# Three more groups of products on zeros, and another written-out order, in a fused state-space and SiLU kernel

## The chip, the cores and the metric

The kernel runs on one core of one Trainium2 chip. The metric is the device time of one execution in microseconds (us), the median of a few runs. A profile of one further execution gives the traces that are read below; its times are counted from the start of its own span.

## The reference

Two blocks follow each other. The first is a chunked state-space scan over 4 batches, 8 heads, 768 steps, 32 values per head and a state of 16; the second is a two-layer network on the 3072 resulting rows of 256 values.

```python
for c in range(nc):                      # chunks of 32 steps
    cum = np.cumsum(log_a[chunk])
    L  = np.exp(cum[i] - cum[j]) * causal
    y  = (C @ B.T * L) @ x + (C @ state) * np.exp(cum)
    state = decay_full * state + sum_j(B_j x_j * decay_from_j)
x = y.transpose(0, 2, 1, 3).reshape(3072, 256)
h = x @ w_in                             # 256 -> 2048
out = (h * sigmoid(h)) @ w_out           # 2048 -> 256
```

All inputs and the output are float32.

## The kernel before

The 3072 rows are cut into 12 units of 256 rows (three per batch, `UT = 256`), and two units make a pair of 512 rows for the network. The kernel has no loop over them. One string, `SCHEDULE`, holds some 1400 tokens; each token calls one small function, which records a few instructions for one engine. The string is the order of the program: every engine gets its instructions in the order in which the tokens stand, and waits at each for the data that it needs. A second table, `SLOTS`, says which of the numbered buffers each new tile gets (49 small ones `s2k`, 12 large ones `r4k`, 7 `raw` for weights as loaded, 3 accumulators `hp`). Nothing else decides order or place.

The scan of one unit u, with the lines of the profile:

- Loads: `Ln` (L244, B and C by rows), `Lt` (L252, four pieces per tensor in the other layout), `Lx` (L259, x), `La` and `Lp` (L219 and L227, decay factors from a scratch tensor in DRAM). The last number of a token is the queue that issues it: 0 is SP's, 1 is ACT's, 2 is POOL's. A DMA waits until the DMA that used its semaphore last has landed; there are eight such semaphores in rotation, so it waits for the one eight places before it.
- Decay: for units 0 and 1, `ab` (L477) spreads the factors by products on TensorE and `E` (L486) scans them on VectorE (DVE); `E,0,0,1`, `E,0,0,0` and `E,0,1` are unit 0, `E,1,1` and `E,1,0` unit 1. `pb` (L451) and `P01` (L456) do the same for another layout; later units use `P` (L463).
- Operands: `B` (L494, POOL), `T` (L499, a transpose on DVE; `T,0,1` makes C of unit 0 from its four `Lt` pieces), `tp` and `tq` (L505 on TensorE and L514 on ScalarE (ACT), a transpose of B), `ce` (L520, ACT), `C` (L525, mostly POOL).
- Products: `D` or `gd` (L547, B times x), `g0` (L561, C times B), then `M` (L576, DVE, times the decay), `b` and `S` (L570 on ACT and L591 on DVE, the state), `SM` (L599, ACT), and `Y` (L612, then L621, the unit's result), which is copied out by `X0` (L651, units 0 and 1) or `y` (L657).

The network: weights come with `lw` (L278) and are cut into a high and a low part over several steps: `u`, `v`, `H` and `Wd` on ACT (L284, L287, L315, L326), `w` and `Wl` on DVE (L293, L297, L300, L321), `W` and `We` on POOL (L311, L330). The first pair of units uses plain float32 products, `s` and `n` (L681 and L749), with `si` (L687) between; the other five pairs use three products of parts, `a` and `d` (L790) and `f` (L771, each `f,1` is one product of 512 columns), with `ax`, `dg`, `h` on ACT (L801, L811, L817) and `l`, `e` on DVE (L638, L641). Rows leave with `o` (L699) and `O` (L703).

The token that the change adds is `z`: `z,1` is one bfloat16 product of a tile of zeros with itself, 128x512, into the bank `o_ps` (L421), and `z,0,6` is six small ones of 64x64 (L423). Their result is read by nobody; the bank is overwritten by the next `tp`.

```python
def busy(n, little=0):
    t = bank("z")
    for i in range(n):
        nc.tensor.matmul(out=t, lhsT=idle[:, 0:128], rhs=idle, start=True, stop=True)
```

Of the kernel before, what the change touches and what calls it, by code (L numbers as in the profile page):

```python
# [30 lines left out]
n,1 W,10,1,0 lw,12 W,5,1,0 M,2,0 Ln,3,0,0,0 w,11,1 P,2 T,3,1 La,3,0,0 C,2 n,1 b,2,0 W,11,1,0 u,6 La,3,1,0 n,1 S,2,0
w,6,0 s,0,5 w,7,2 Wd,0 b,2,1 Lx,3,1,0 S,2,1 Lt,4,1,0,0 v,6 n,1 Ln,3,0,1,0 u,7 w,7,0 Lt,3,0,1,0 S,2,2 AD,1 ce,3,1 w,7,1
SM,2,0 w,6,1 n,1 H,5 SM,2,1 Lt,3,0,0,0 Lt,3,0,2,0 Lt,3,0,3,0 n,1 Y,2 Lx,3,0,0 si,0,5 w,6,2 E,3,0 E,3,1 y,2,0 W,7,1,0
B,3 u,12 T,3,0 Lp,3,0 n,1 w,12,0 n,1 ce,3,0 H,11 y,2,1 lw,13 La,4,0,0 Lt,4,0,2,0 W,6,1,0 Lt,4,1,2,0 w,12,1 s,0,7 g0,3
gd,3 si,0,7 H,3 s,0,6 b,3,0 P,3 Wl,0 H,7 n,1 M,3,1 Lt,4,1,3,0 Wl,2 S,3,0 La,4,1,0 b,3,1 n,1 S,3,1 v,12 xh,2 si,0,6
S,3,2 Lt,4,0,1,0 Wd,4 Lt,4,0,0,0 x,2,1 M,3,0 s,1,6 Lt,4,1,1,0 SM,3,1 S,3,3 SM,3,0 Lx,4,1,0 C,3 x,2,0 H,6 si,1,6 lw,15
lw,14 Ln,4,0,1,0 w,12,2 W,12,1,0 T,4,1 H,9 Y,3 Ln,4,0,0,0 s,1,5 E,4,1 n,1 u,13 y,3,1 y,3,0 H,8 v,13 xh,3 Lt,4,0,3,0
n,1 Lx,4,0,0 u,15 w,13,0 x,3,0 si,1,5 We,0 a,1,0 AD,2 Lp,4,0 s,1,7 x,3,1 ce,4,0 v,14 ax,1,0 w,13,2 w,13,1 d,1,0 u,14
H,10 n,1 La,5,1,0 w,14,2 W,13,1,0 ce,4,1 n,1 E,4,0 B,4 T,4,0 dg,1,0 Wd,2 Wd,5 g0,4 Lt,5,1,2,0 La,5,0,0 w,14,0 w,14,1
gd,4 b,4,0 b,4,1 Wl,9 P,4 Wd,3 C,4 S,4,0 M,4,0 Wd,10 Lx,5,0,0 S,4,1 w,15,0 M,4,1 Lp,5,0 Lt,5,1,1,0 S,4,2 n,1 W,14,1,0  # L40
v,15 H,14 Lt,5,1,3,0 SM,4,0 n,1 Wl,10 SM,4,1 H,13 Wd,9 n,1 si,1,7 Wl,3 n,1 w,15,2 Wd,1 w,15,1 Y,4 n,2 y,4,0 a,1,2 Wl,1
Ln,5,0,0,0 We,2 h,1,0 n,1 Lt,5,1,0,0 n,1 ax,1,2 y,4,1 e,1,0 W,15,1,0 Wd,8 a,1,1 We,1 La,6,0,0 n,2 Wl,8 We,9 xh,4 n,1
l,1,0 ax,1,1 T,5,1 H,12 f,2 d,1,2 Lt,5,0,1,0 dg,1,2 We,8 d,1,1 dg,1,1 Vn,0 n,1 a,1,4 a,1,3 Lt,5,0,2,0 f,1 Vn,1 S,4,3
f,4 P,5 h,1,1 Wl,5 f,1 Wl,14 We,4 x,4,0 We,10 Ln,5,0,1,0 La,6,1,0 ce,5,0 E,6,0 Lt,5,0,0,0 ax,1,4 ax,1,3 Lx,5,1,0
Lt,6,1,0,0 Wl,12 d,1,4 We,3 Wl,11 Lt,5,0,3,0 x,4,1 d,1,3 T,5,0 f,1 h,1,2 ce,5,1 E,5,0 E,5,1 C,5 Lt,6,1,1,0 f,1 dg,1,4
Lt,6,0,2,0 Lt,6,1,2,0 f,1 e,1,1 f,1 Lt,6,0,3,0 f,1 Lt,6,1,3,0 Lt,6,0,0,0 Lt,6,0,1,0 l,1,1 f,1 B,5 dg,1,3 H,15 g0,5
T,6,1 gd,5 M,5,1 AD,3 Wd,7 We,5 f,1 ce,6,0 b,5,0 f,1 h,1,3 Ln,6,0,1,0 f,1 S,5,0 b,5,1 Ln,6,0,0,0 e,1,2 S,5,1 S,5,2 f,1
Wl,7 a,1,5 M,5,0 l,1,2 f,1 Lp,6,0 h,1,4 f,2 Lt,7,1,2,0 ax,1,5 f,2 Wd,6 f,1 Wd,11 l,1,3 d,1,5 f,1 SM,5,1 f,1 dg,1,5
o,0,0,2 P,6 Wl,6 We,7 f,1 Wd,12 e,1,3 ce,6,1 f,2 l,1,4 f,3 We,11 f,1 We,12 SM,5,0 Y,5 f,1 Lx,6,1,0 T,6,0 Lt,7,1,1,0
f,1 ct y,5,1 E,6,1 Lx,6,0,0 f,1 a,1,7 Lx,7,0,0 e,1,4 f,2 B,6 f,2 y,5,0 Ln,7,0,1,0 ax,1,7 f,1 C,6 f,1 h,1,5 We,6 xh,5  # L50
d,1,7 f,1 Wl,15 f,1 dg,1,7 o,0,1,2 f,1 Lt,7,0,2,0 Wd,15 f,1 Lx,7,1,0 gd,6 Lt,7,1,3,0 g0,6 f,2 M,6,1 x,5,0 Wd,14 Wl,13
f,1 x,5,1 f,1 O,0,0,2,0,0 f,2 b,6,0 b,6,1 M,6,0 f,1 h,1,7 a,2,1 l,1,5 ax,2,1 a,1,6 Wd,13 Lp,7,0 S,6,0 Lt,7,0,0,0 d,2,1
Lt,7,1,0,0 f,1 e,1,5 Lt,7,0,1,0 We,13 f,1 S,6,1 ax,1,6 dg,2,1 l,1,7 La,7,1,0 T,7,1 d,1,6 dg,1,6 ce,7,0 f,1 S,6,2
SM,6,0 f,2 SM,6,1 f,2 h,1,6 f,1 Y,6 l,1,6 S,6,3 f,3 y,6,0 f,1 e,1,6 Lt,8,1,0,0 ce,7,1 P,7 f,3 y,6,1 We,15 La,7,0,0 f,1
# [836 lines left out]
```

## Time and profile before

| what | us |
|---|---|
| median of three runs | 329.32 |
| the three runs | 331.9, 329.31, 329.32 |
| the profiled execution | 327.4 |
| its span in the trace | 325.7 |
| TensorE (PE) busy in the span | 319.0 |
| VectorE (DVE) busy | 235.2 |
| ScalarE (ACT) busy | 207.4 |
| GpSimd (POOL) busy | 69.3 |

The profiled execution lasted 1.7 us longer than its span, which begins with the first instruction and ends with the last. "PEld" is TensorE's loading of stationary operands, which runs beside its products. A product with float32 operands leaves two records, one with bfloat16 or with split parts one. The order of instructions comes from the tokens, so a row of the trace can be matched with its token by line and position.

### The profile page before, as it was taken

What the parts mean: (1) busy time and instruction counts of PE and PEld (TensorE: products, weight loads), DVE (VectorE), ACT (ScalarE), POOL (GpSimd) and SP (SyncE); (2) the same over time, 40 slices, a digit from 0 to 9 for tenths busy, and PEclk for the clock granted to TensorE, in tenths of its full rate; (3) what the DMA queues carried; (4) which work ended last, traced back from release to release, by engine and by line L of the source; (5) the groups of instructions that cost most, each with busy time, mean ns of one, the idle gap of its engine ahead of it and who ended that gap; (6) DMA issues with size and microseconds to landing.
All of it is one profiled execution on the core that took longest, in us unless ns stands there. A gap on an engine that the chain in (4) does not pass through costs nothing.

```text
span 325.7 us, 7539 instructions
## 1 busy us (share of the span) xinstructions
PE 319.0 (98%) x3065; PEld 243.7 (75%) x3065; DVE 235.2 (72%) x330; ACT 207.4 (64%) x321; POOL 69.3 (21%) x88
## 2 busy tenths in 40 slices
PE   8899999999999999999999999999999999999995
PEld 4578656665677777877777878778887888888883
DVE  7968989798987986769386768886567563366373
ACT  2869665877499678655567667645856464864441
POOL 6447375335741422100000101010010000000000
PEclk9999999999999999999999999999999999999999
DMA  7899986945947669340604153143001100003002
GB/s 149 192 318 216 232 184 180 213 122 115 206 82 117 107 136 180 72 70 4 133 16 78 51 112 64 38 82 74 2 0 27 33 0 0 2 13 60 17 1 64
DMA packets 95762, 30.64 MB, mean 94 GB/s; under 512 B 80280, under 2 KB 86936, under 8 KB 95728
## 3 DMA queue, kind: packets, MB, share of 16 engines
q1 hardware_dynamic: 90576, 25.38, 35.7%
q0 software_dynamic: 2480, 4.39, 7.6%
q10 hardware_dynamic: 2672, 0.39, 0.7%
q8 instruction: 24, 0.39, 0.5%
q14 instruction: 10, 0.08, 0.1%
HBM read 22.61 MB, written 3.34 MB: 80 GB/s over the span
## 4 chain that ended last, share of the span: by engine, by line
PE 90%; DVE 3%; DMA 2%; ACT 2%; POOL 1%; issue 1%; POOLq 0%; DVEq 0%
PE hp L771 29%; PE gb L790 17%; PE ga L790 16%; PE hp L681 7%; PE hp L749 7%; PE o_ps L771 6%; DMA s2k<-in_B_dram 2%; PE ga L621 2%; PE ga L561 2%; PE ga L612 2%; PE gb L612 1%; PE ga L547 1%; DVE ab L486 1%; DVE ab L576 0%; DVE s2k L300 0%
## 5 line engine op out<-in xcount | busy, mean ns | idle before, releaser
L771 PE MATMUL hp<-r4k,s2k 128*128 128x512 f32 x400 | 112.9, 394 | 0.0
L771 PEld LDWEIGHTS hp<-r4k,s2k 128*128 128x128 f32 x400 | 74.3, 188 | 16.3 <-issue 0.8
L638 DVE SCALAR_TENSOR_TENSOR r4k<-r4k,r4k 128x1024 fp32r<-128x1024 f32 x40 | 48.7, 1221 | 31.4 <-ACT r4k L817 23.7
L790 PE MATMUL ga<-raw,s2k 128*128 128x512 f32 x240 | 62.7, 396 | 0.0
L641 DVE SCALAR_TENSOR_TENSOR r4k<-r4k,r4k 128x1024 fp32r<-128x1024 f32 x40 | 48.6, 1219 | 19.2 <-ACT r4k L817 13.3
L790 PE MATMUL gb<-raw,s2k 128*128 128x512 f32 x240 | 61.4, 391 | 0.0
L790 PEld LDWEIGHTS ga<-raw,s2k 128*128 128x128 f32 x240 | 44.5, 188 | 11.6 <-issue 0.7
L790 PEld LDWEIGHTS gb<-raw,s2k 128*128 128x128 f32 x240 | 44.7, 188 | 10.6 <-ACT ys L657 0.6
L817 ACT ACTIVATE r4k<-r4k 128x1024 fp32r<-128x1024 f32 x40 | 41.8, 1056 | 2.0 <-DVE r4k L641 1.0
L494 POOL TENSOR_TENSOR BT<-bn,ab 128x256 f32<-128x256 f32 x10 | 10.4, 1042 | 104.4 <-DVE ab L486 83.9
L811 ACT ACTIVATE r4k<-ga 128x1024 f32<-128x1024 f32 x20 | 20.5, 1026 | 18.2 <-PE ga L790 17.5
L801 ACT ACTIVATE ga<-ga 128x1024 f32<-128x1024 f32 x20 | 20.2, 1009 | 18.4 <-PE ga L790 18.4
L801 ACT ACTIVATE gb<-gb 128x1024 f32<-128x1024 f32 x20 | 20.2, 1009 | 18.3 <-PE gb L790 18.3
L771 PE MATMUL o_ps<-r4k,s2k 128*128 128x512 f32 x80 | 31.0, 394 | 0.0
L681 PE MATMUL hp<-r4k,s2k 128*128 128x256 f32 x128 | 29.6, 383 | 0.6 <-ACT r4k L651 0.6
L311 POOL TENSOR_TENSOR s2k<-s2k,s2k 128x512 uint32<-128x512 uint32 (+1 forms) x19 | 24.6, 1300 | 25.3 <-DVE s2k L300 13.8
L749 PE MATMUL hp<-r4k,s2k 128*128 128x512 f32 x64 | 29.8, 598 | 0.0
L486 DVE TENSOR_TENSOR_SCAN ab<-ab,diag 128x512 f32<-128x512 f32 x20 | 27.1, 1372 | 2.9 <-DMA ab<-az 2.9
L681 PEld LDWEIGHTS hp<-r4k,s2k 128*128 128x128 f32 x128 | 23.9, 190 | 5.4 <-issue 1.4
L811 ACT ACTIVATE r4k<-gb 128x1024 f32<-128x1024 f32 x20 | 20.5, 1024 | 6.3 <-PE gb L790 4.5
L749 PEld LDWEIGHTS hp<-r4k,s2k 128*128 128x128 f32 x64 | 11.7, 189 | 10.4 <-issue 9.6
L330 POOL DMA_DIRECT2D s2k<-s2k x16 | 14.2, 1090 | 15.9 <-ACT s2k L326 7.0
(120 smaller groups left out, 382.2 us busy)
## 6 DMA issues: line engine op xcount, KB each, us to landing
ab<-az SPq DMA_DIRECT2D x20, 256.0 KB, 5.5
raw<-in_moe_w_in_dram SPq DMA_DIRECT2D x8, 512.0 KB, 5.1
raw<-in_moe_w_out_dram SPq DMA_DIRECT2D x8, 512.0 KB, 5.9
s2k<-s2k POOLq DMA_DIRECT2D x16, 256.0 KB, 4.7
out_dram<-r4k SPq DMA_DIRECT2D x44, 64.0 KB, 1.8
xt<-in_x_dram SPq DMA_DIRECT2D x20, 128.0 KB, 4.8
pz<-ac SPq DMA_DIRECT2D x10, 130.0 KB
bn<-in_B_dram SPq DMA_DIRECT2D x20, 64.0 KB, 2.5
```

The source lines that it names most:

```text
L311: nc.gpsimd.tensor_tensor(out=dst[:, :, fs].bitcast(U32), in0=u[:, :, fs], in1=v[:, :, fs], op=ALU.add)
L330: nc.gpsimd.dma_start(out=f32(WK[n, p]).rearrange("p k f -> p (k f)"), in_=other.rearrange("p k f -> p (k f)"), accum_op=ALU.add)
L486: nc.vector.tensor_tensor_scan(out=o, data0=src, data1=heads(diag, half).rearrange("p h t -> p (h t)"), initial=0.0, op0=ALU.mult, op1=ALU ...
L638: nc.vector.scalar_tensor_tensor(out=l, in0=f32(h), scalar=BACK, in1=y, op0=ALU.mult, op1=ALU.add)
L641: nc.vector.scalar_tensor_tensor(out=d, in0=f32(h), scalar=-(BACK + 1.0), in1=y, op0=ALU.mult, op1=ALU.subtract)
L681: nc.tensor.matmul(out=hp[:, i], lhsT=WT[j][:, kc, 128 * i:128 * i + 128], rhs=XM[:, 2 * kc:2 * kc + 2, u], start=(kc == 0), stop=(kc == K ...
L749: nc.tensor.matmul(out=NP["o"][m], lhsT=WT[8 + f // 2][:, f % 2, 128 * m:128 * m + 128], rhs=GT[0, f // 2][:, f % 2], start=(f == 0), stop ...
L771: nc.tensor.matmul(out=ACC[P, 2 * (p == "d") + m], lhsT=WK[8 + f // 2, p][:, f % 2, 128 * m:128 * m + 128], rhs=rhs, start=(f == 0 and p ! ...
L790: nc.tensor.matmul(out=o, lhsT=WK[j, q][:, kc, 128 * i:128 * i + 128], rhs=xs[:, 2 * kc:2 * kc + 2], start=(start and q == "h" and kc == 0 ...
L801: nc.scalar.activation(t, t, AF.Copy, scale=1.0 + Z)
L811: nc.scalar.activation(g, t, AF.Silu, scale=BACK)
L817: nc.scalar.activation(t, GT[G, i], AF.Copy, scale=-LESS * Z)
```

## The change

The tokens stand in another order, and three `z,1` are added; every other token is there as often as before (the `f` and `n` groups are cut differently, with the same sums, 480 and 32 products). `SLOTS` gives the tiles other buffers accordingly. The last 485 tokens, from `h,3,1` on, are the same in both.

The beginning before and after, and the two places of `Wl,4`:

```diff
-ch ci cs zr Ln,0,0,0,1 cP cI z,1 z,1 z,1 ia ip,0 z,0,6 Lt,0,1,0,1 c1 cp z,0,6 z,1 A,1 c2 A,0 Lt,0,1,3,1 Lt,0,1,2,1
-PA,0 Lt,0,1,1,1 ab,0,0,1 ab,0,0,0 ab,0,1 Lx,0,1,0 cd Ln,0,0,1,1 PA,1 E,0,0,1 lw,2 u,2 co E,0,0,0 E,0,1 pb,0 T,0,1
-ce,0,0 P01,0 Lx,0,0,0 ce,0,1 B,0,0 B,0,1 z,1 lw,1 ab,1,1 E,1,1 tp,0 tq,0 D,0 g0,0 S,0,0 lw,0 w,2,0 S,0,1 Ln,1,0,0,0
-v,2 M,0,1 u,1 M,0,0 z,0,6 C,0 Ln,1,1,0,0 z,0,6 Ln,1,1,1,0 Ln,1,0,1,0 S,0,2 v,1 w,2,1 SM,0,0 Lx,1,0,0 SM,0,1 ab,1,0
-Lx,1,1,0 w,2,2 lw,3 W,2,2,0 Y,0 u,0 ir,3 W,2,2,1 ir,1 X0,0,0 X0,0,1 lw,4 v,0 ir,0 s,0,2 E,1,0 S,0,3 si,0,2 tp,1 ce,1,0
...
-w,9,0 Ln,2,0,1,0 W,3,1,0 AA,1 s,0,3 La,2,1,0 s,1,3 H,2 La,2,0,0 W,8,1,0 v,10 Wl,4 w,5,0 u,11 Lx,2,1,0 v,9 w,5,1 si,0,3
...
-gd,4 b,4,0 b,4,1 Wl,9 P,4 Wd,3 C,4 S,4,0 M,4,0 Wd,10 Lx,5,0,0 S,4,1 w,15,0 M,4,1 Lp,5,0 Lt,5,1,1,0 S,4,2 n,1 W,14,1,0
+ci cs ia ch ip,0 c1 Ln,0,0,0,1 z,1 cp z,1 zr c2 Lt,0,1,1,1 A,1 z,1 Lt,0,1,2,1 cI Lt,0,1,3,1 z,0,6 z,0,6 Lt,0,1,0,1 z,1
+PA,0 A,0 cP cd ab,0,0,1 ab,0,0,0 E,0,0,1 E,0,0,0 Lx,0,1,0 ab,0,1 Ln,0,0,1,1 T,0,1 E,0,1 pb,0 ab,1,1 PA,1 B,0,0 B,0,1
+P01,0 ce,0,1 ce,0,0 lw,2 E,1,1 z,1 Lx,0,0,0 lw,1 z,1 tp,0 u,2 tq,0 v,2 C,0 D,0 lw,0 S,0,0 g0,0 z,0,6 z,0,6 w,2,0 S,0,1
+Ln,1,1,0,0 M,0,1 M,0,0 Ln,1,0,0,0 Ln,1,0,1,0 S,0,2 Ln,1,1,1,0 u,1 w,2,2 v,1 SM,0,0 w,2,1 SM,0,1 u,0 Lx,1,0,0 Lx,1,1,0
+lw,3 ab,1,0 Y,0 ir,2 W,2,2,0 lw,4 W,2,2,1 E,1,0 ir,1 B,1,0 ir,3 X0,0,0 z,1 z,1 w,0,0 X0,0,1 v,0 w,1,0 B,1,1 s,0,2 ir,0
...
+La,5,0,0 gd,4 w,14,0 w,14,1 Wd,3 b,4,0 Wl,4 b,4,1 Wl,9 P,4 C,4 n,1 W,14,1,0 M,4,1 S,4,0 M,4,0 Lx,5,0,0 S,4,1 Lp,5,0
```

Read engine by engine, the beginning is this. TensorE before: three `z,1`, two `z,0,6`, `z,1`, `ab,0,0,1`, `ab,0,0,0`, `ab,0,1`, `pb,0`, `z,1`, `ab,1,1`, `tp,0`, `D,0`, `g0,0`, two `z,0,6`, `ab,1,0`, `Y,0`, `s,0,2`. After: the same, but `ab,1,1` stands right behind `pb,0`, two `z,1` stand between it and `tp,0`, and two more stand between `Y,0` and `s,0,2`. On DVE the order before is `E,0,0,1 E,0,0,0 E,0,1 T,0,1 P01,0 E,1,1 S,0,0 w,2,0 S,0,1 M,0,1 M,0,0`; after, `T,0,1` stands ahead of `E,0,1`. On ACT the two `ce` of unit 0 come ahead of `u,2`, and the four `Lt` pieces of unit 0 are issued in another order, in the same four places of the queue. The first seven DMAs of SP's queue are the same. Between there and the common tail, some 60 tokens on DVE, 70 on ACT, 15 on TensorE, 10 on POOL and 60 on SP's queue stand a few places earlier or later; `Wl,4` moves from the weights of the first pair to just ahead of `Wl,9` and `P,4`, and `M,4,1` moves ahead of `S,4,0`.

## The prediction

> **What bounds the kernel now.** I read the busy shares first, then the chain that ended last, then TensorE by stages.
>
> ```profile
> PE 319.0 (98%) x3065; PEld 243.7 (75%) x3065; DVE 235.2 (72%) x330; ACT 207.4 (64%) x321; POOL 69.3 (21%) x88
> ...
> PE 90%; DVE 3%; DMA 2%; ACT 2%; POOL 1%; issue 1%; POOLq 0%; DVEq 0%
> ```
>
> ```profile
> 9.20:14.00 4.80, 4.15 (x167) 2.81 (x167) 4.60 (x11) 3.97 (x10) 1.71 (x4) 1.00 0.91 179
> 14.00:60.00 46.00, 45.92 (x527) 32.45 (x528) 40.15 (x71) 33.49 (x70) 25.06 (x26) 1.00 0.89 219
> 60.00:80.00 20.00, 19.86 (x301) 12.60 (x300) 17.00 (x26) 16.27 (x33) 8.91 (x9) 1.00 0.66 150
> 80.00:165.00 85.00, 84.98 (x790) 65.67 (x788) 65.58 (x84) 58.21 (x88) 22.82 (x24) 1.00 0.58 109
> ```
>
> The first number pair of the windows is the stretch, then TensorE's busy time. From 14 us on TensorE idles 0.08 us up to 60, 0.14 up to 80, 0.02 up to 165, and nothing shows until 316: it is the bound, and the amount of its work there is not changed (480 and 480 products of parts, 64 and 32 plain ones). An order of the other engines can lose time there, but gain hardly any. What can be gained lies before 14 us, and that stage is a chain of latencies:
>
> ```profile
> 0.82 2.62 DMA s2k<-in_B_dram
> 3.44 0.02 issue
> 3.46 5.26 DMA s2k<-in_B_dram
> 8.72 0.04 issue
> 8.77 0.33 PE o_ps L505
> ```
>
> The second half of B lands at 8.72 us; TensorE's `tp,0` waits for it, then `D,0` (9.18), `g0,0` (9.64), DVE's `M` (10.51), `Y,0` (11.85), ACT's `X0` (13.40) and `s,0,2` (13.93) follow. From `s,0,2` on TensorE is dense, so a shift of that instruction shifts the end by as much. Both transfers of B keep their places in ACT's queue, so 8.72 stands.
>
> **The change part by part.**
>
> *The zeros cost nothing.* One `z,1` at full speed takes TensorE 0.22 us (6.73 to 6.95 in the rows below).
>
> ```profile
> 6.73 0.39 PE L421 MATMUL o_ps<-s2k 128*128 128x512 bf16 x1
> 6.95 1.02 PE L477 MATMUL hp<-s2k,s2k 128*128 128x512 f32 x2
> 7.81 0.27 PE L505 MATMUL o_ps<-ident,s2k 128*128 128x128 f32 x1
> 8.77 0.33 PE L505 MATMUL o_ps<-ident,s2k 128*128 128x128 f32 x1 [0.68 <-DMA s2k<-in_B_dram]
> ```
>
> After the change `ab,1,1` starts at 6.73 instead of 6.95, ends its turn at 7.59, two zeros take it to 8.04, and the first transpose moves from 7.81 to 8.04. The second still waits for 8.72: 0.68 us of idle time covers the 0.23. If B landed at 7.8 the cost would be 0.23. The other two stand behind `Y,0`, whose last product is issued at 13.16; they take the engine to about 13.65, inside the 0.55 us in which `s,0,2` waits for `X0` (13.38 to 13.93). Cover gone, they would cost 0.45; at half speed (three zeros from 1.27 to 2.66 are 0.46 each) they would take 0.9 and cost about 0.4. I take 0 for both.
>
> *The transpose ahead of `E,0,1` costs about 0.4 us.* These are DVE's rows:
>
> ```profile
> 4.91 2.51 DVE L486 TENSOR_TENSOR_SCAN ab<-hp,diag 128x256 f32<-128x256 f32 x3 [0.28 <-PE hp L477]
> 7.34 0.63 DVE L499 STREAM_TRANSPOSE ct<-s2k 128x256 f32<-128x256 f32 x1
> 7.81 0.63 DVE L456 TENSOR_TENSOR_SCAN s2k<-hp,s2k 128x260 f32<-128x260 f32 x1
> 8.37 1.19 DVE L486 TENSOR_TENSOR_SCAN ab<-hp,diag 128x512 f32<-128x512 f32 x1
> 9.73 0.23 DVE L589 COPY st<-hp 128x64 f32<-128x64 f32 x1 [0.17 <-PE hp L547]
> ```
>
> The first two scans end at 6.18. `T,0,1` needs all four pieces of C, issued by ACT from 1.33 to 2.92. When the last lands is seen on SP's queue: the seventh DMA behind it, `Ln,1,1,0,0`, reuses its semaphore and starts only at 6.78, though the one before it was issued from 5.81 to 6.29. Today the transpose comes at 7.34, when that is past. In its new place it waits until about 6.8. From there the spacings of these rows give: `E,0,1` at 6.8 + 0.47 = 7.27 (6.20 before), `P01,0` 1.14 later at 8.41, `E,1,1` 0.56 later at 8.97, its end 1.19 later at 10.16. `S,0,0` came at 9.73; it now comes at 10.1 to 10.16. Behind it stand `w,2,0`, `S,0,1`, `M,0,1` and `M,0,0` with no gap, and TensorE's `Y,0` waits for `M` with nothing useful to do. So `Y,0`, `X0` and `s,0,2` come about 0.4 later, and the end with them. `B,0,1` on POOL needs `E,0,1` (8.46 now), still ahead of B's 8.72; the `ce` of unit 0 come earlier. From the other side: if the last piece landed with the median of its kind (2.7 us after 2.92, so 5.6), the transpose would follow the scans at once, `E,1,1` would end at about 9.5 and the cost would be 0. I take 0.4, because SP's row is nearer to the thing itself than a median.
>
> *`Wl,4` in unit 4 costs nothing.* It puts 0.6 us (the spacing of L321, 71.26 to 71.86) ahead of `P,4` on DVE.
>
> ```profile
> 71.86 0.69 DVE L463 TENSOR_TENSOR_SCAN pfx<-pz,one 128x260 f32<-128x260 f32 x1
> 73.40 1.32 DVE L591 SCALAR_TENSOR_TENSOR st<-st,pfx,bxs 128x64 f32<-128x64 f32 x1 [0.84 <-ACT bxs L570]
> ```
>
> Behind `P,4` DVE idles 0.84 for ACT's `b,4,0`. That covers it, and `M,4,1`, moved into that gap, no longer stands behind `S,4,1` and `w,15,0`, so both `M` end no later than the 76.45 of today, when `Y,4` waits for them. TensorE loses 0.14 there (77.52, for `SM`); at most that comes back, and if the cover fails 0.6 is lost. I take -0.1.
>
> *The other moves* I price at 0. They pass over one to three neighbours of 0.2 to 1.2 us on engines that are busy 40.15 of 46.00 (DVE) and 33.49 (ACT) between 14 and 60 us; TensorE's moved tokens only change places with products of equal price. The trace cannot show a wait that isn't there yet. Two steps of the dearest kind (`l`, 1.22 us) arriving late would be 2.4 us lost; nothing below -0.2 is to be had, since TensorE idles no more than that.
>
> *Sum:* 0 + 0.4 - 0.1 + 0 = 0.3 us. The profiled execution goes from 327.4 to 327.7, its span from 325.7 to 326.0. The median of the timed runs, 329.32, stands 1.9 above the profiled execution; I carry the same shift over to it: **329.6**.
>
> The zeros are meant for the clock, so that is weighed here. The granted clock is 1.00 in every window up to 316 us, but the products show a slow start: zeros 0.46 apart from 1.27 on, 0.22 at 6.73. `ab,0,0,1`, `ab,0,0,0` and `ab,0,1` (1024 columns) took 3.84 to 6.09, 2.25 us, where 512 columns later took 0.86 (6.95 to 7.81); so some 1.1 us of that ran at half speed, and full speed began at about 4.9. No idle gap of TensorE before 14 us is longer than 0.68. [...]
>
> **The rivals.**
>
> *A, slow start in the timed runs.* The timed runs are 1.9 us longer than the profiled one, and no trace shows where. If full speed came only at about 8 instead of 4.9, the products would run on at 0.43 per 256 columns: `ab,0,1` would end near 7.3 and `E,0,1`, which needs it, start at 7.4. `T,0,1` at 6.8 then fills DVE's idle time instead of standing behind `E,0,1`, and its 0.47 (7.34 to 7.81) comes off the same chain. That gives 329.32 - 0.5 = 328.8. For it: the size of the gap fits. Against: the only trace shows 4.9. [...]
>
> *B, the zeros do what they are for.* If the 1.9 us are a stretch of half speed later in the first 14 us (3.8 us at half speed lose 1.9), and three more zeros prevent it, the median falls to 327.4. For it: the same 1.9. Against: at most 0.68 us of idle time to fill.
>
> *C, slower.* The transpose waits on DVE for its last piece, at a price of 1 for 1 from the point where that lands after 6.4. With the latency of the B transfer behind it in the same queue (5.26 us) it would land at 2.92 + 5.26 = 8.2 and cost 1.8: 331.2. With a late step of 2.4 us beside it, 333. For it: that queue's latencies rise from 2.6 to 5.3. Against: SP's 6.78.
>
> **How the numbers follow.** Forecast (329.0 to 330.3): 0.58. A: 0.17, B: 0.12, C: 0.13. 1% is 3.3 us, about what a measurement of this kernel can tell from no change. Faster by over 1% means under 326.0, which is under the profiled execution of before and needs B and more: 0.04. Slower by over 1%, over 332.6, needs C with its late step: 0.06. Within 1%: 0.90. The range, 327.2 to 331.2, takes in A, B and C's first price, and so the bounds of the unknown costs but for two late steps.
>
> **What would show it.** `T,0,1` at about 6.8 behind an idle gap that a DMA of C ends; `M,0,1` at about 10.9, `s,0,2` at about 14.3; the two zeros ahead of `tp,0` inside the wait for B; no idle of TensorE over 0.2 between 18 and 316. I am wrong if `s,0,2` starts at 13.9 or earlier, if the spacing of the early zeros changes with the run, or if new waits stand between 18 and 165.

## The result

The changed kernel takes 328.52 us (median of 22 runs, 327.7 to 331.43); the kernel before, run beside it, 330.52 (22 runs, 328.15 to 334.71). The ratio is 0.995, with a 95% interval of 0.9927 to 0.9973: it is faster by 0.3 to 0.7%, where the prediction had it slower by 0.1%. (The ratios of this document leave out executions that were more than 1.5% above the fastest of their kernel, and in the experiments all of these had lost the clock, as told below; the medians are of all.) The 329.32 from which the prediction started was the median of only three runs, and the profiled execution beside it, 327.40, was faster than all 22 runs above.

So the two profiles disagree with the medians: the profiled execution of the changed kernel took 328.53, 1.1 **longer** than that of the kernel before, with a span of 326.8 against 325.7. That contradiction is what the experiments had to settle.

### The profile after

The busy shares and the chain that ended last:

```profile
PE 320.4 (98%) x3068; PEld 244.3 (75%) x3068; DVE 235.6 (72%) x330; ACT 208.2 (64%) x321; POOL 68.0 (21%) x88
...
PE 96%; ACT 1%; issue 1%; DVE 1%; DVEq 0%
```

TensorE has the three products more (3068 for 3065) and is as dense as before. The start, first on VectorE, then on TensorE (start, length, engine, line and operation, then what ended the idle time):

```profile
6.86 0.64 DVE L499 STREAM_TRANSPOSE ct<-s2k 128x256 f32<-128x256 f32 x1 [0.39 <-DMA s2k<-in_C_dram]
7.35 1.16 DVE L486 TENSOR_TENSOR_SCAN ab<-hp,diag 128x512 f32<-128x512 f32 x1
...
9.02 1.20 DVE L486 TENSOR_TENSOR_SCAN ab<-hp,diag 128x512 f32<-128x512 f32 x1
10.14 0.19 DVE L589 COPY st<-hp 128x64 f32<-128x64 f32 x1
...
10.77 0.68 DVE L576 TENSOR_TENSOR ab<-gb,ab 128x512 f32<-128x512 f32 x1
```

```profile
3.84 3.11 PE L477 MATMUL hp<-s2k,s2k 128*128 128x256 f32 x6
...
7.51 1.12 PE L477 MATMUL hp<-s2k,s2k 128*128 128x512 f32 x2
8.47 0.59 PE L421 MATMUL o_ps<-s2k 128*128 128x512 bf16 x2
8.90 0.38 PE L505 MATMUL o_ps<-ident,s2k 128*128 128x128 f32 x2
...
13.57 0.60 PE L421 MATMUL o_ps<-s2k 128*128 128x512 bf16 x2
14.19 0.67 PE L681 MATMUL hp<-r4k,s2k 128*128 128x256 f32 x2
```

`T,0,1` waits until 6.86 for a piece of C, as foreseen; `E,0,1` follows at 7.35, `S,0,0` at 10.14, the first `M` at 10.77, `s,0,2` at 14.19 (13.93 before). The zeros at 13.57 stand in the wait for `X0`. Those at 8.47 stand in no wait. The three `ab` of unit 0 (L477) take 3.11 us in this execution, 2.32 before: by the clock record full speed begins at 6.3 here, at 4.7 there. So TensorE reaches the zeros without a gap, and the transposes come behind them at 8.90, though B had landed at 7.23 (8.72 before). VectorE covers these 0.43 us: the last `g0` on TensorE ends at 10.45, and VectorE, without a gap from 6.86 on, comes to the first `M` only at 10.77.

In unit 4, VectorE:

```profile
73.82 0.69 DVE L463 TENSOR_TENSOR_SCAN pfx<-pz,one 128x260 f32<-128x260 f32 x1
74.43 0.66 DVE L576 TENSOR_TENSOR ab<-gb,ab 128x512 f32<-128x512 f32 x1
75.01 0.43 DVE L591 SCALAR_TENSOR_TENSOR st<-st,pfx,bxs 128x64 f32<-128x64 f32 x1
```

`M,4,1` (L576) now fills the wait in front of the state update. And the stages, with TensorE's busy time behind the length of each:

```profile
9.20:14.00 4.80, 4.54 (x169) 2.80 (x168) 4.80 (x10) 3.75 (x9) 1.42 (x3) 1.00 0.70 92
14.00:60.00 46.00, 44.85 (x523) 31.54 (x523) 37.47 (x65) 32.35 (x68) 25.98 (x28) 1.00 0.79 207
60.00:80.00 20.00, 20.00 (x303) 13.11 (x302) 19.47 (x32) 17.42 (x36) 7.97 (x9) 1.00 0.75 163
80.00:165.00 85.00, 85.00 (x787) 65.32 (x786) 65.83 (x83) 58.89 (x88) 22.20 (x24) 1.00 0.58 112
```

Between 14 and 60 us TensorE now idles 1.15 us, where the profile of before had 0.08. Most of it is one hole, in the middle of `Y,1`; TensorE's timeline there:

```profile
20.92 0.33 PE L612 MATMUL gb<-ab,s2k 64*32 64x64 f32 x10
22.15 0.27 PE L612 MATMUL gb<-ab,s2k 64*32 64x64 f32 x2 [0.90 <-issue]
22.35 0.27 PE L621 MATMUL ga<-cw,sm 32*64 32x64 f32 x2
```

Ten of the last twelve products of a group run, then nothing for 0.90 us, then the last two. They are parts of one group with the same operands, and "issue" says that TensorE waited for nothing that the profile shows.

### The same hole in the kernel before

One more profiled execution of the **kernel before** (run e7, below) has a hole as well. Its timeline, then three windows of equal length; the granted clock is the third number from the end:

```profile
21.78 0.24 PE L621 MATMUL ga<-cw,sm 32*64 32x64 f32 x1
23.46 0.27 PE L621 MATMUL ga<-cw,sm 32*64 32x64 f32 x2 [1.45 <-issue]
```

```profile
20.75:24.16 3.41, 1.96 (x99) 1.45 (x97) 2.39 (x6) 2.28 (x5) 1.45 (x3) 1.00 0.98 339
24.16:27.57 3.41, 3.41 (x8) 2.75 (x9) 1.02 (x3) 2.31 (x5) 1.47 (x3) 0.50 0.90 202
27.57:30.98 3.41, 3.41 (x17) 2.99 (x16) 0.61 (x3) 1.45 (x3) 1.26 (x1) 1.00 1.02 284
```

TensorE stands 1.45 us, and right behind that its clock is granted at half for 3.41 us: 8 products where the next window has 17. That costs another 1.7 us. This execution took 331.45 us, 4.05 more than the first profiled one, which had no hole and no half speed behind it. The hole and the half speed make 3.15 of that; another 0.8 stands ahead of them, where full speed began at 7.1 instead of 4.7 and `s,0,2` at 14.71 instead of 13.93.

What TensorE waits for can be inferred from the DMA queues. One queue of the page is called "instruction" and moves 24 packets of 16 KB. Its second packet, in e7 (two stretches of time; packets, MB and share of 16 engines' time):

```profile
q1 hardware_dynamic: 3838, 1.68, 94.9%
...
q1 hardware_dynamic: 283, 0.30, 86.2%
q8 instruction: 1, 0.02, 5.5%
```

The first line is 14.0 to 21.2 us: data alone, and the sixteen engines all but full. The other two are 21.2 to 22.3: the packet is there, from 21.27 to 22.23, and TensorE goes on 1.23 us later. TensorE has 6,136 products and weight loads in the changed program, some 256 for each of the 24 packets; and in the eight of the twelve profiled executions of this study in which it stops, it stops at the same place of its stream, between its 704th and 706th record. With the three more products that is the last pair of L612; without them, the first pair of L621.

All twelve profiled executions, in order of the hole. "Idle in its window" is TensorE's idle time in the 3.41 us window that held most of the hole, counted from the moment at which that execution's clock record begins full speed; half speed at the very start and at the very end of an execution is left out:

| kernel | second packet in, us | hole, us | idle in its window | half speed after it | execution, us |
|---|---|---|---|---|---|
| e6: before, more instructions | 16.99 | 0 | | no | 327.19 |
| e10: after, both | 18.10 | 0 | | no | 327.79 |
| e8: after, more instructions | 18.13 | 0 | | no | 327.47 |
| before, first profile | 18.46 | 0 | | no | 327.40 |
| e2: after without the zeros | 21.00 | 0.34 | 0.36 | no | 328.43 |
| after | 20.82 | 0.90 | 0.90 | no | 328.53 |
| e9: before, one load later | 20.46 | 1.09 | 0.66 | no | 328.50 |
| e7: before again | 22.23 | 1.45 | 1.45 | 3.41 us | 331.45 |
| e4: after, transposition back | 22.92 | 1.93 | 1.90 | 3.41 us | 332.15 |
| e3: before, transposition first | 22.37 | 2.00 | 1.12 | no | 330.38 |
| e1: before with the zeros | 22.65 | 2.43 | 2.28 | 3.41 us | 332.05 |
| e5: after, one load earlier | 23.35 | 3.21 | 2.68 | 6.83 us | 333.88 |

The hole ends 1.2 to 1.5 us after the packet is in, in all eight executions that have one; with the packet in before 18.5 there is none.

### The profile page after: what moved, and what is told of

It is laid out like the page before. It is cut to its first block, busy times and chain, and to the rows that moved or that the text cites. A ratio compares the mean times of both kernels' runs of the same rounds, so it can differ in the third digit from the quotient of the medians.

```text
span 326.8 us, 7551 instructions
## 1 busy us (share of the span) xinstructions
PE 320.4 (98%) x3068; PEld 244.3 (75%) x3068; DVE 235.6 (72%) x330; ACT 208.2 (64%) x321; POOL 68.0 (21%) x88
## 4 chain that ended last, share of the span: by engine, by line
PE 96%; ACT 1%; issue 1%; DVE 1%; DVEq 0%
PE hp L771 29%; PE ga L790 17%; PE gb L790 17%; PE hp L749 9%; PE hp L681 8%; PE o_ps L771 6%; PE ga L561 2%; PE ga L621 2%; PE ga L612 2%; PE gb L612 1%; PE hp L477 1%; PE ga L547 1%; PE o_ps L421 1%; PE gb L561 0%; ACT L687 0%
## 5 line engine op out<-in xcount | busy, mean ns | idle before, releaser
L638 DVE SCALAR_TENSOR_TENSOR r4k<-r4k,r4k 128x1024 fp32r<-128x1024 f32 x40 | 50.0, 1251 | 30.9 <-ACT r4k L817 21.7
L641 DVE SCALAR_TENSOR_TENSOR r4k<-r4k,r4k 128x1024 fp32r<-128x1024 f32 x40 | 49.0, 1229 | 17.7 <-ACT r4k L817 11.0
L790 PEld LDWEIGHTS gb<-raw,s2k 128*128 128x128 f32 x240 | 44.8, 188 | 10.9 <-ACT ys L657 0.6
L494 POOL TENSOR_TENSOR BT<-bn,ab 128x256 f32<-128x256 f32 x10 | 9.0, 900 | 101.6 <-DVE ab L486 53.5
L486 DVE TENSOR_TENSOR_SCAN ab<-ab,diag 128x512 f32<-128x512 f32 x20 | 27.1, 1376 | 3.3 <-DMA ab<-az 2.6
```

The source lines that it names most:

```text
L486: nc.vector.tensor_tensor_scan(out=o, data0=src, data1=heads(diag, half).rearrange("p h t -> p (h t)"), initial=0.0, op0=ALU.mult, op1=ALU ...
L638: nc.vector.scalar_tensor_tensor(out=l, in0=f32(h), scalar=BACK, in1=y, op0=ALU.mult, op1=ALU.add)
L641: nc.vector.scalar_tensor_tensor(out=d, in0=f32(h), scalar=-(BACK + 1.0), in1=y, op0=ALU.mult, op1=ALU.subtract)
L790: nc.tensor.matmul(out=o, lhsT=WK[j, q][:, kc, 128 * i:128 * i + 128], rhs=xs[:, 2 * kc:2 * kc + 2], start=(start and q == "h" and kc == 0 ...
```

## The experiments

Each was timed in five rounds beside the kernel before, except e7. The first four go by three theories: Z says that the zeros make the gain, T the transposition, O the rest of the order. "Lost the clock" counts the timed runs with a mean granted clock of 0.995 or less (half speed over 3.41 us of some 329 takes 0.005 off the mean; half speed at the very end takes up to 0.003 off, as in the profile of e3, 0.997).

| run | median, us (runs) | before beside it | ratio, 95% | lost the clock |
|---|---|---|---|---|
| after | 328.52 (22) | 330.52 (22) | 0.995 (0.9927 to 0.9973) | 1 of 22 |
| e1 | 329.82 (12) | 330.33 (35) | 0.9979 (0.9939 to 1.0019) | 4 of 12 |
| e2 | 328.77 (12) | 330.33 (35) | 0.9957 (0.9922 to 0.9993) | 1 of 12 |
| e3 | 331.84 (12) | 330.33 (35) | 1.0023 (0.9984 to 1.0063) | 7 of 12 |
| e4 | 328.79 (12) | 330.33 (35) | 0.9949 (0.9913 to 0.9985) | 1 of 12 |
| e5 | 331.58 (12) | 330.21 (29) | 1.002 (0.9978 to 1.0062) | 9 of 12 |
| e6 | 327.74 (12) | 330.21 (29) | 0.9925 (0.989 to 0.996) | 1 of 12 |
| e8 | 327.66 (12) | 330.21 (29) | 0.9957 (0.9926 to 0.9988) | 0 of 12 |
| e9 | 328.75 (12) | 329.67 (23) | 0.9971 (0.9935 to 1.0008) | 3 of 12 |
| e10 | 327.92 (12) | 329.67 (23) | 0.9941 (0.9915 to 0.9966) | 0 of 12 |

The kernel before lost the clock in 17 of 35, 13 of 29 and 7 of 23 runs. In the 35, the median was 332.17 of those that did and 329.38 of those that did not.

### e1: the zeros alone

The kernel before with the three `z,1` where the change has them.

```diff
-ce,0,0 P01,0 Lx,0,0,0 ce,0,1 B,0,0 B,0,1 z,1 lw,1 ab,1,1 E,1,1 tp,0 tq,0 D,0 g0,0 S,0,0 lw,0 w,2,0 S,0,1 Ln,1,0,0,0
+ce,0,0 P01,0 Lx,0,0,0 ce,0,1 B,0,0 B,0,1 z,1 lw,1 ab,1,1 z,1 E,1,1 tp,0 tq,0 D,0 g0,0 S,0,0 lw,0 w,2,0 S,0,1 Ln,1,0,0,0
...
-Lx,1,1,0 w,2,2 lw,3 W,2,2,0 Y,0 u,0 ir,3 W,2,2,1 ir,1 X0,0,0 X0,0,1 lw,4 v,0 ir,0 s,0,2 E,1,0 S,0,3 si,0,2 tp,1 ce,1,0
+Lx,1,1,0 w,2,2 lw,3 W,2,2,0 Y,0 u,0 ir,3 W,2,2,1 ir,1 X0,0,0 z,1 z,1 X0,0,1 lw,4 v,0 ir,0 s,0,2 E,1,0 S,0,3 si,0,2 tp,1 ce,1,0
```

> The kernel before with only the three added groups of zeros (one more ahead of tp,0, two behind Y,0), every other token where it was. Theory Z (the zeros keep the clock up through the early waits, and that is the whole gain): the median falls by about 2 us, to 328.5, and the runs draw together as those of the changed kernel do (327.7 to 331.4 against 328.2 to 334.7). Theory T (the transpose ahead of E,0,1 shortens DVE's early chain where full speed comes late): no change, 330.5 with the wide spread. Theory O (the rest of the searched order gains it): no change, 330.5.

Measured: 329.82, ratio 0.9979, an interval that holds 1. Its profile has a hole of 2.43 us and half speed behind it. The zeros did not keep the clock (4 of 12 runs lost it), and make at most a part of the gain.

### e2: everything but the zeros

The changed kernel without its three added `z,1`.

```diff
-P01,0 ce,0,1 ce,0,0 lw,2 E,1,1 z,1 Lx,0,0,0 lw,1 z,1 tp,0 u,2 tq,0 v,2 C,0 D,0 lw,0 S,0,0 g0,0 z,0,6 z,0,6 w,2,0 S,0,1
+P01,0 ce,0,1 ce,0,0 lw,2 E,1,1 z,1 Lx,0,0,0 lw,1 tp,0 u,2 tq,0 v,2 C,0 D,0 lw,0 S,0,0 g0,0 z,0,6 z,0,6 w,2,0 S,0,1
...
-lw,3 ab,1,0 Y,0 ir,2 W,2,2,0 lw,4 W,2,2,1 E,1,0 ir,1 B,1,0 ir,3 X0,0,0 z,1 z,1 w,0,0 X0,0,1 v,0 w,1,0 B,1,1 s,0,2 ir,0
+lw,3 ab,1,0 Y,0 ir,2 W,2,2,0 lw,4 W,2,2,1 E,1,0 ir,1 B,1,0 ir,3 X0,0,0 w,0,0 X0,0,1 v,0 w,1,0 B,1,1 s,0,2 ir,0
```

> The changed kernel without its three added groups of zeros, every other token as in it. Theory Z: back to about 330.5 with the wide spread. Theory T and theory O: it stays at about 328.5 and narrow.

Measured: 328.77, ratio 0.9957 with an interval below 1. Without the zeros the gain is there; theory Z falls.

### e3 and e4: the transposition

e3 is the kernel before with `T,0,1` ahead of `E,0,1`; e4 the changed kernel with it back behind.

```diff
-PA,0 Lt,0,1,1,1 ab,0,0,1 ab,0,0,0 ab,0,1 Lx,0,1,0 cd Ln,0,0,1,1 PA,1 E,0,0,1 lw,2 u,2 co E,0,0,0 E,0,1 pb,0 T,0,1
+PA,0 Lt,0,1,1,1 ab,0,0,1 ab,0,0,0 ab,0,1 Lx,0,1,0 cd Ln,0,0,1,1 PA,1 E,0,0,1 lw,2 u,2 co E,0,0,0 T,0,1 E,0,1 pb,0
```

> The kernel before with only T,0,1 moved ahead of E,0,1. Theory T: the median falls by 0.5 or more, towards 329.5. Theory Z: not faster; by the recorded prediction 0.4 slower in a run that has full speed by 4.9 us, so 330.5 to 331. Theory O: 330.5. The transpose is seen to wait until about 6.8 in every theory.

```diff
-PA,0 A,0 cP cd ab,0,0,1 ab,0,0,0 E,0,0,1 E,0,0,0 Lx,0,1,0 ab,0,1 Ln,0,0,1,1 T,0,1 E,0,1 pb,0 ab,1,1 PA,1 B,0,0 B,0,1
+PA,0 A,0 cP cd ab,0,0,1 ab,0,0,0 E,0,0,1 E,0,0,0 Lx,0,1,0 ab,0,1 Ln,0,0,1,1 E,0,1 T,0,1 pb,0 ab,1,1 PA,1 B,0,0 B,0,1
```

> The changed kernel with T,0,1 put back behind E,0,1. Theory T: slower than the changed kernel by 0.5, about 329. Theory Z and theory O: 328.1 to 328.5, the same as the changed kernel or up to 0.4 faster.

Measured: 331.84 (1.0023, an interval that holds 1) and 328.79 (0.9949, below 1). Alone it gains nothing, and without it the gain stays: theory T falls, O is left. But O is no cause: it names some 200 moved tokens. The four traces had one thing in common, the hole in `Y,1`, of another length each time, and behind the two of them with more than 1.9 us of idle time in one window a stretch of half speed.

From here on the theory was **F**: TensorE comes to the end of the instructions it holds, the next packet stands behind big weight loads on the DMA engines, and when the hole is long the clock falls back as well. The change moved the weight loads. SyncE's queue in the kernel before (first profile) and after; `raw` are the big weight loads, 512 KB each:

```profile
15.91 0.39 SPq L278 DMA_DIRECT2D raw<-in_moe_w_in_dram  x1
16.35 0.43 SPq L356 DMA_DIRECT2D s2k<-in_a_dram  x1
16.82 0.39 SPq L278 DMA_DIRECT2D raw<-in_moe_w_out_dram  x1
```

```profile
15.05 0.37 SPq L278 DMA_DIRECT2D raw<-in_moe_w_in_dram  x1
15.46 1.45 SPq L356 DMA_DIRECT2D s2k<-in_a_dram  x3
16.95 0.39 SPq L244 DMA_DIRECT2D tbc<-in_C_dram  x1
17.38 2.37 SPq L278 DMA_DIRECT2D raw<-in_moe_w_out_dram  x3
```

Before, two big loads go out within 0.9 us, at 15.91 and 16.82. After, four small ones stand between the first and the next, which goes out 2.3 us later. When the packet is asked for is not recorded; it is inferred from its earliest starts, in e6 and e8, with TensorE's 464th and 472nd record begun. So it is asked for at about the 455th to 470th, and TensorE is there at some 17 us.

### e5: one weight load earlier, in the changed kernel

```diff
-lw,3 ab,1,0 Y,0 ir,2 W,2,2,0 lw,4 W,2,2,1 E,1,0 ir,1 B,1,0 ir,3 X0,0,0 z,1 z,1 w,0,0 X0,0,1 v,0 w,1,0 B,1,1 s,0,2 ir,0
-S,0,3 tp,1 Ln,2,1,0,0 w,1,1 si,0,2 pb,1 w,0,1 ce,1,0 lw,9 w,0,2 ce,1,1 D,1 tq,1 lw,8 P01,1 g0,1 S,1,0 S,1,1 lw,10 v,3
+lw,3 ab,1,0 Y,0 ir,2 W,2,2,0 lw,4 W,2,2,1 lw,9 E,1,0 ir,1 B,1,0 ir,3 X0,0,0 z,1 z,1 w,0,0 X0,0,1 v,0 w,1,0 B,1,1 s,0,2 ir,0
+S,0,3 tp,1 Ln,2,1,0,0 w,1,1 si,0,2 pb,1 w,0,1 ce,1,0 w,0,2 ce,1,1 D,1 tq,1 lw,8 P01,1 g0,1 S,1,0 S,1,1 lw,10 v,3
```

> The changed kernel with one SyncE issue moved: lw,9 (one of the big weight loads) goes out ahead of ir,1, ir,3, ir,0 and the Ln loads that it stood behind. Nothing on TensorE, VectorE or ScalarE is moved and its data are needed no earlier. Theory F (fetch: TensorE comes to the end of the instructions it holds in the middle of Y,1, and goes on when the second packet of its instruction queue is in; that packet stands behind weight loads on the DMA engines): the packet lands later than the 20.8 us of the changed kernel's profile, towards 22 to 22.9, the stall in Y,1 grows from 0.9 towards 2 us, more executions lose the full clock, and the median goes from 328.5 to 329.5 to 331. Theory O (the other moves of the order gain by themselves, by what each engine does next): nothing that an engine waits for is changed, 328.5 as before, within 0.4.

Measured: 331.58, 3.1 above the changed kernel, with 9 of 12 runs losing the clock instead of 1 of 22. F had 329.5 to 331; the packet and the hole went further than it said, to 23.35 and 3.21 us. `lw,9` went out at 16.48, in the profile of the changed kernel at 17.38. The timeline of TensorE and the windows:

```profile
21.20 0.33 PE L612 MATMUL gb<-ab,s2k 64*32 64x64 f32 x10
24.74 0.37 PE L612 MATMUL gb<-ab,s2k 64*32 64x64 f32 x2 [3.21 <-issue]
```

```profile
20.80:24.21 3.41, 0.73 (x62) 0.57 (x61) 2.22 (x5) 1.52 (x4) 2.07 (x4) 1.00 1.10 322
24.21:27.62 3.41, 2.88 (x38) 2.32 (x38) 0.00 (x0) 1.42 (x4) 1.43 (x3) 0.50 0.79 217
27.62:31.04 3.42, 3.42 (x10) 2.70 (x9) 1.46 (x3) 2.03 (x6) 1.26 (x1) 0.50 1.02 277
```

One issue moved by about 1 us, whose data are needed no earlier, takes away the whole gain of the change. Theory O, by which no engine's work is touched and so nothing changes, is refuted.

### e6: TensorE further in its stream, in the kernel before

Two groups of small products on zeros (`z,0,12`, `z,0,10`) in idle time. The 44 of the text below are instructions: 22 products with a weight load each, against three products and three loads in e1.

```diff
-ce,0,0 P01,0 Lx,0,0,0 ce,0,1 B,0,0 B,0,1 z,1 lw,1 ab,1,1 E,1,1 tp,0 tq,0 D,0 g0,0 S,0,0 lw,0 w,2,0 S,0,1 Ln,1,0,0,0
+ce,0,0 P01,0 Lx,0,0,0 ce,0,1 B,0,0 B,0,1 z,1 lw,1 ab,1,1 z,0,12 E,1,1 tp,0 tq,0 D,0 g0,0 S,0,0 lw,0 w,2,0 S,0,1 Ln,1,0,0,0
...
-Lx,1,1,0 w,2,2 lw,3 W,2,2,0 Y,0 u,0 ir,3 W,2,2,1 ir,1 X0,0,0 X0,0,1 lw,4 v,0 ir,0 s,0,2 E,1,0 S,0,3 si,0,2 tp,1 ce,1,0
+Lx,1,1,0 w,2,2 lw,3 W,2,2,0 Y,0 u,0 ir,3 W,2,2,1 ir,1 X0,0,0 z,0,10 X0,0,1 lw,4 v,0 ir,0 s,0,2 E,1,0 S,0,3 si,0,2 tp,1 ce,1,0
```

> The kernel before with two groups of products on zeros at the places where the change has its three groups' idle time (z,0,12 ahead of tp,0, z,0,10 behind Y,0): about the same busy time as in the run with the three groups, but 44 small products in place of 6 large ones, so TensorE is some 40 instructions further in its stream at every later moment. Theory F (fetch): the second instruction packet is asked for at some 15.5 us instead of 17 to 17.6, ahead of the weight loads, lands before TensorE needs it, the stall in Y,1 (2 us in most executions) is gone, hardly any execution loses the full clock, and the median is 328 to 329 (ratio to the kernel before 0.992 to 0.997), though no step of the program is in another place. If busy time on zeros is what counts: like the run with the three groups, 329.8 (0.998). If neither counts: 330.5 (1.000).

Measured: 327.74, ratio 0.9925, and 1 of 12 losing the clock: 2.5 below the kernel before, which is more than the whole change gains, with no step of the program in another place. The packet started at 15.79 and was in at 16.99, and TensorE passes the place without a stop:

```profile
20.62 0.34 PE L612 MATMUL gb<-ab,s2k 64*32 64x64 f32 x12
20.95 0.27 PE L621 MATMUL ga<-cw,sm 32*64 32x64 f32 x2
20.96 0.27 PE L621 MATMUL gb<-cw,sm 32*64 32x64 f32 x2
```

e1 had zeros in the same two places, and its 0.5 lies inside its interval. What tells the two runs apart is how many instructions the zeros are, 44 in e6 and 6 in e1, and the second packet, in at 16.99 and at 22.65: so what counted here is how many instructions were behind TensorE when the packet was asked for.

### e7: the kernel before once more

> The kernel before once more, for one more profiled execution. Theory F: the profile of the kernel before that was shown (no stall in Y,1, its second instruction packet in at 18.46 us) is the lucky one; here the packet lands after 20.7 us and TensorE stands 0.5 to 2.5 us at the first product of L621 or the last of L612 behind it; span 326 to 330.5. If the fetch is no matter of the execution: no stall, packet in at 18.5, span 325.7 within 0.3.

Measured: the hole of 1.45 us at the first products of L621 and half speed behind it, shown above. The first profile of the kernel before was a lucky one: its packet began at 17.45, this one's at 21.27.

### e8: the same groups in the changed kernel

They stand in place of the three `z,1` that the change added.

```diff
-P01,0 ce,0,1 ce,0,0 lw,2 E,1,1 z,1 Lx,0,0,0 lw,1 z,1 tp,0 u,2 tq,0 v,2 C,0 D,0 lw,0 S,0,0 g0,0 z,0,6 z,0,6 w,2,0 S,0,1
+P01,0 ce,0,1 ce,0,0 lw,2 E,1,1 z,1 Lx,0,0,0 lw,1 z,0,12 tp,0 u,2 tq,0 v,2 C,0 D,0 lw,0 S,0,0 g0,0 z,0,6 z,0,6 w,2,0 S,0,1
...
-lw,3 ab,1,0 Y,0 ir,2 W,2,2,0 lw,4 W,2,2,1 E,1,0 ir,1 B,1,0 ir,3 X0,0,0 z,1 z,1 w,0,0 X0,0,1 v,0 w,1,0 B,1,1 s,0,2 ir,0
+lw,3 ab,1,0 Y,0 ir,2 W,2,2,0 lw,4 W,2,2,1 E,1,0 ir,1 B,1,0 ir,3 X0,0,0 z,0,10 w,0,0 X0,0,1 v,0 w,1,0 B,1,1 s,0,2 ir,0
```

> The changed kernel with z,0,12 and z,0,10 in place of its three z,1 groups (the same two idle times, the same busy time within 0.3 us, some 40 more instructions). Theory F (fetch): the stall of 0.9 us in Y,1 goes, the median is 327.5 to 328.2 (0.3 to 0.9 below the changed kernel's 328.5). Theory O without the fetch: 328.5 as the changed kernel, within 0.3. If the large products on zeros count for the clock: 328.5 or above.

Measured: 327.66, no run losing the clock, all twelve between 327.3 and 328.68. The medians of it and of e6 lie below those of both kernels of the comparison, though neither was timed beside the changed kernel. And with the hole out of the way the two orders, timed in the same rounds, are equal, 327.74 and 327.66: of the changed order, nothing else that a median shows is left.

### e9: one weight load later, in the kernel before

`lw,8` stands just ahead of `lw,10`, as in the changed kernel.

```diff
-tq,1 w,1,0 w,0,0 ce,1,1 pb,1 w,0,2 lw,8 B,1,0 w,0,1 B,1,1 W,0,2,0 w,1,1 D,1 P01,1 S,1,0 g0,1 W,0,2,1 S,1,1 M,1,0
-Lt,3,1,1,0 M,1,1 ir,2 S,1,2 s,0,0 SM,1,1 w,1,2 SM,1,0 W,1,2,0 C,1 ca W,1,2,1 lw,10 AA,0 si,0,0 Y,1 u,3 u,4 w,3,0
+tq,1 w,1,0 w,0,0 ce,1,1 pb,1 w,0,2 B,1,0 w,0,1 B,1,1 W,0,2,0 w,1,1 D,1 P01,1 S,1,0 g0,1 W,0,2,1 S,1,1 M,1,0
+Lt,3,1,1,0 M,1,1 ir,2 S,1,2 s,0,0 SM,1,1 w,1,2 SM,1,0 W,1,2,0 C,1 ca W,1,2,1 lw,8 lw,10 AA,0 si,0,0 Y,1 u,3 u,4 w,3,0
```

> The kernel before with one SyncE issue moved the other way: lw,8 (a big weight load, issued at 16.8 us) goes out just ahead of lw,10 (19.3 us), as it does in the changed kernel. Nothing on TensorE is moved or added. Theory F (fetch): the second instruction packet, asked for at 17 to 17.6 us, has only lw,4 and small loads ahead of it, lands at 19.5 to 21 instead of 21 to 23 us, the stall in Y,1 is 0 to 1 us instead of some 2, fewer executions lose the full clock, and the median is 328.5 to 329.3 (ratio 0.994 to 0.997): this one move makes most of what the whole change gave. Theory O2 (something else of the searched order also gains, and e6 was fast for its small products): 330.2, within 0.4.

Measured: 328.75, inside what F said, with 3 of 12 losing the clock against 7 of 23 beside it. But the interval of the ratio reaches 1.0008, and the edit did less than it was to do: `lw,8` went out at 16.96, behind two small transfers and not at 19.3. The packet was in at 20.46 and the hole 1.09 us, slightly over the 0 to 1 that F gave. This supports F and does not decide; e5 and e6 do.

### e10: and the start as it was

e8 with `T,0,1` back behind `E,0,1`, the edit of e4.

> The changed kernel with the 44 small products on zeros in place of its three z,1 groups and with T,0,1 back behind E,0,1 (so the start does not wait for the fourth piece of C). If the start's wait is worth what the profile of the changed kernel showed (0.26 us) and the stall in Y,1 stays gone: 327.2 to 327.5, 0.1 to 0.4 below the run that only has the small products (327.66). If the start costs nothing in most executions: 327.7.

Measured: 327.92, against e8's 327.66 in other rounds. No gain of moving the transposition back is to be seen in timed runs.

## Why the prediction was wrong

The forecast was 329.6, a change of +0.3; measured were 328.52 and a change of -2.0. The time lay in the range, and within 1% of before, but on the other side; that it lay in the range was luck, since the lower end of the range was set by rival B, whose cause is not the one found. For the second point below, these are VectorE's rows of two executions, with `E,0,1` in L486 and the transposition in L499: of the kernel before, with full speed from 7.1 (e7), and of the changed order, with full speed from 4.5 (e8).

```profile
7.38 1.22 DVE L486 TENSOR_TENSOR_SCAN ab<-hp,diag 128x512 f32<-128x512 f32 x1 [0.90 <-PE hp L477]
8.52 0.62 DVE L499 STREAM_TRANSPOSE ct<-s2k 128x256 f32<-128x256 f32 x1
```

```profile
7.14 0.64 DVE L499 STREAM_TRANSPOSE ct<-s2k 128x256 f32<-128x256 f32 x1 [1.06 <-DMA s2k<-in_C_dram]
7.63 1.16 DVE L486 TENSOR_TENSOR_SCAN ab<-hp,diag 128x512 f32<-128x512 f32 x1
```

Point by point:

- **The zeros, 0.** Right in size, as far as the runs can tell, but not for the reason given. The two at 13.57 stand in the wait that was named. The first pair does not: in the profile of the changed kernel there is no wait for B left, and VectorE is what covers them. Alone (e1) the zeros move the median by 0.5, inside the interval; without them (e2) it is 0.25 higher, in other rounds.
- **The transposition, +0.4.** The wait was seen rightly: it lasted until 6.86 (foreseen 6.8), the first `M` came at 10.77 (10.9), `s,0,2` at 14.19 (14.3). But that this is 0.26 later than before is not its price, and the agreement is in part luck: full speed began later in this execution, and `E,0,1` could not have started before 6.95, when its products ended. What the transposition does depends on that start. In e7's rows above, `E,0,1` waits for TensorE, and a transposition ahead of it would have filled that time. In e8's, it stands behind the transposition, which waits for C. With full speed by 4.7, `s,0,2` came at 13.54 to 13.93 with the transposition behind (before, e6, e9), at 14.47 and 14.56 with it ahead (e8, e2). With full speed from 6.3 on, it came at 14.61 to 15.29 with it behind (e7, e1, e4), at 14.19 and 14.47 with it ahead (after, e5). In between, 5.6 and 5.9, it made no difference (14.53 in e10, 14.55 in e3). So by these profiles, which differ in other tokens too, it costs some 0.5 to 1.0 after an early start of full speed and costs nothing after a late one. No median (e3, e4, e10) shows either.
- **Unit 4, -0.1.** Right: TensorE was busy 20.00 of 20 us there, 19.86 before.
- **The other moves, 0.** This is the step that failed, with its bound: "nothing below -0.2 is to be had, since TensorE idles no more than that". The bound was read from one execution in which, by luck, the second instruction packet came early. In the other profiles with its first part in that order (e7, e1, e3) TensorE idled 1.45 to 2.43 us in one hole between 21 and 25 us, and in 37 of 87 timed runs its clock fell back. SyncE's queue was looked at as loads that could be late, not as traffic that something else stands behind.
- **"I carry the same shift over to it."** This failed with it. The 1.9 us between the profiled execution and the median were for the most part that hole and what it does to the clock, and the change acts on it: e6, the same order without the hole, has a median of 327.74. Executions of before without loss of the clock had a median of 329.38, those of the changed kernel 328.52: 0.9 less. And of before, 17 of 35 lost the clock and took 2.8 more, which is 1.4 in the mean, against 1 of 22. Together that is 2.2 or so; the means of the comparison differ by 2.3 (331.05 and 328.75).
- **Rival A**, the late start of full speed, was right that the moment differs, and about the mechanism: full speed began between 4.2 and 7.2 us in the twelve profiles, and where it began late, `E,0,1` did wait for its products (at half speed 256 columns take 0.86, the two records of a product starting 0.43 apart, at 3.84, 4.26 and 4.69 in the profile of the changed kernel, and not the 0.43 of its text; its 7.3 goes by 0.86, and e7 had 7.34). But its 0.5 is not what the medians show: with the hole gone, the orders with the transposition ahead and behind have 327.66 and 327.74. That its 328.8 lies near the 328.52 is luck.
- **Rival B**, a stretch of half speed of some 3.8 us that goes away, was right about the size and the kind (3.41 us, -1.7), and wrong about place and cure: it lies at 24 us, far behind the start, and the zeros do not prevent it.
- **Rival C**: the last piece of C landed before 6.9 in the profile of the changed kernel; no price of 1.8. (Its sums are 331.1 and, with the late step, 333.5.)
- Of the things that were to prove it wrong, "new waits between 18 and 165" came true: the hole of 0.90. By its own test the forecast would have called that a loss; it is the short form of a hole that the kernel before has at greater length, 1.45 in e7.

**What stays open:** why the packet of the kernel before came early in one profile and late in another, at nearly the same load; whether TensorE's clock falls back by the idle share of a window alone (below); and which of the moves on SyncE's queue counts most. One rival was not tested: the four profiles whose clock fell back behind the hole are the four in which full speed began last, at 6.9 to 7.2 us. The windows are counted from that moment, so it sets whether a window's end cuts the hole, and a late start may decide whether a hole costs the clock. No run sets that moment. That the packets of that queue are TensorE's is inferred, from their number, from the fixed place of the stop and from e6, where more instructions on TensorE alone moved them.

## What to carry to other kernels

A gap of the bound engine that the profile puts down to "issue", in the middle of a group with the same operands, is worth a look at the DMA queue called "instruction": in the eight profiles with such a gap here, of 0.34 to 3.21 us, it ended 1.2 to 1.5 us after the second packet of that queue was in, though no wait of the program is to be seen. With one bulk load that nobody needed yet issued 0.9 us earlier, the packet was in at 23.35 instead of 20.82 and the median 3.1 longer (e5); with 22 tiny products in early idle time it was in at 16.99 and the median 2.5 shorter (e6). So issuing such a load later, or a few tiny instructions ahead, is worth trying where such a gap shows. And where the profiled execution is faster than all timed runs, a second profile is needed before anything is priced: the difference may be the very thing that the change acts on.

## What the runs showed of the hardware

**Instruction packets.** The queue whose packets are taken here for TensorE's moved 24 of 16 KB, in the mean one for some 256 of the 6,136 products and weight loads. TensorE stopped at its 704th to 706th record when the second was late, and went on 1.2 to 1.5 us after it was in; the hole was up to 3.21 us. The first packet started at record 217 to 221 in the eight profiles with a hole. How many instructions TensorE holds was not measured. An estimate from these counts: if the first packet brought the 256 of the mean, the other 450 or so of the 705 were there without any packet of this queue.

**The clock fell back after less than a full window of idling.** The clock records of these executions change in steps of 3.41 us, and the windows go by that: half speed lasted 3.41 us in e7 and 6.83, twice that, in e5; in both it began 17.07 us, five times that, after full speed did (7.09 to 24.16 and 7.14 to 24.21), and in the first profiles of both kernels full speed lasted 320.85 us, 94 times 3.413. After windows with 1.45, 1.90, 2.28 and 2.68 us of idle time around the hole, of 3.41 us each, the next window ran at half speed; after 1.12 or less a clock at full speed stayed there. The ends of the spans, where TensorE's work runs out, give more cases: the clock stayed up after a window with 1.36 us idle (e4) and fell back after one with 1.87 (e3).

```profile
324.63:328.04 3.41, 2.05 (x9) 1.15 (x8) 1.60 (x6) 0.98 (x2) 0.00 (x0) 1.00 0.45 77
328.04:330.43 2.39, 0.00 (x0) 0.00 (x0) 0.00 (x0) 0.00 (x0) 0.00 (x0) 1.00 0.37 110
```

```profile
323.35:326.76 3.41, 1.54 (x7) 0.74 (x5) 1.31 (x5) 0.74 (x2) 0.00 (x0) 1.00 0.57 114
326.76:328.64 1.88, 0.00 (x0) 0.00 (x0) 0.00 (x0) 0.00 (x0) 0.00 (x0) 0.50 0.24 71
```

A clock that is already at half is another case: in e5 it stayed there for a second window after one with 0.53 us idle. e3 had the third longest hole, 2.00 us, and kept its clock behind it: a window's end cut it in two. Its windows there:

```profile
19.57:22.98 3.41, 2.29 (x71) 1.59 (x70) 2.49 (x7) 2.28 (x5) 1.45 (x3) 1.00 0.89 277
22.98:26.39 3.41, 2.54 (x40) 2.26 (x41) 0.92 (x3) 1.79 (x5) 1.75 (x3) 1.00 1.05 303
```

Where a window begins differs between executions, as the start of full speed does (4.2 to 7.2 us). If the idle time in the window is what counts, the limit lies between 1.36 and 1.45 us here; so few cases don't show that nothing else counts.
